# First samples loaded by phase, first taps by column halves, fewer direct outputs

## The chip, the cores and the metric

The kernel runs on one core of a Trainium2 chip. The metric is the time of one execution on the device in microseconds; a smaller one is better. Five engines work beside each other, each through its own queue of instructions in order: TensorE (PE), VectorE (DVE), ScalarE (ACT), GpSimd (POOL) and SyncE (SP), which only issues DMAs here. They wait for each other, and for DMAs, by semaphores.

## The reference

Inputs are `x` (2, 4000, 512), two convolutions' weights `w1` and `w2` (5, 512, 512), `g` (2, 8, 512) and three 512 x 512 matrices, all bfloat16.

```python
xp = jnp.pad(x, ((0,0),(2,2),(0,0)))
h = sum(einsum("btc,cd->btd", xp[:, i:i+T, :], w1[i]) for i in range(5))
h = gelu(h)[:, ::2, :]                       # 2000 positions a batch
hp = jnp.pad(h, ((0,0),(2,2),(0,0)))
f = sum(einsum("btc,cd->btd", hp[:, i:i+T1, :], w2[i]) for i in range(5))
f = gelu(f)[:, ::2, :]                       # 1000 positions a batch
fe = einsum("btd,de->bte", f, w_f)
ge = einsum("bud,de->bue", g, w_g)
j = tanh(fe[:, :, None, :] + ge[:, None, :, :])
return einsum("btud,dv->btuv", j, w_o)       # (2, 1000, 8, 512)
```

Only every second output of a convolution is kept. Output t of the first one is therefore made of five taps on the samples 2t-2 to 2t+2: taps 0, 2 and 4 read even samples, taps 1 and 3 read odd ones.

## The kernel before

Channels lie on the partitions in four blocks of 128, positions along the free dimension. The program is one long list of operations (`pl.op`, `pl.dma`), each with what it reads and writes and an estimated cost. `Plan.schedule` puts the list in order by simulating the engines with these costs, trying several hundred variants of the priorities on ACT and DVE; `Plan.emit` writes each engine's queue in that order and sets the waits. So an edit to a few operations can move others on DVE and ACT far from it. DMAs keep the order in which they stand in the list, and nearly all stand on SP's queue.

**First convolution, batch 0.** The outputs are made in two ways.

- *Direct*: the first `ND` = 438 outputs are the plain sum of five taps (`direct`, L778). The samples for it come untransposed: `load_xr` (L529, L533) loads blocks of 512 samples, four successive samples to a partition, 512 KB for the first block and 384 KB for the second. `turn` (L600, L609) transposes them on PE, 128 columns at a time, for one block `rt` and one phase `pp` (0 even, 1 odd), and DVE (L618) or ACT (L499) copies the result from PSUM into `eo`, which holds even and odd samples apart. Then each tap needs 16 matmuls (4 blocks of output channels by 4 of input channels), done in two pieces for taps 0, 4 and 2, columns up to 254 first and the rest when the second block is there, and in one piece for taps 1 and 3. The order of the taps is `TAPS = (0, 4, 2, 1, 3)`.
- *Triples* (`class Triple`, `class Unit`): three neighbouring outputs at a time out of 9 products and not 15, on sums and differences of sample planes and of weights. The first triple job of batch 0 covers `NF` = 186 triples (planes `xa` and `row`), the second 336 (`xp`); batch 1 has two of 334. The planes are loaded by transposing DMAs (`load_x6`, L543), one for each of six phases. ACT (L499) and DVE (L494) build the sums of planes, and `w1part` (L621, L494, L499) the sums of weights, `w_x` and `w_t`. It works in slices of 128 output channels, and its first step for a slice needs taps 0 and 4.

**After that** the second convolution runs on the same triples, then `fe` and `ge`, then ACT's tanh and the last matrix product. That is done in blocks of four tiles with seven products for eight (`class Seven`) and a few plain tiles (`class Plain`, L1063). Outputs leave as DMAs from SP and, at the very end, from ACT.

**The start.** PE first does `NWARM` = 7 matmuls on zeros. SP issues the first block of samples, tap 0, tap 4, then the second block when the first has landed, tap 2 when tap 0 has landed, and then `xa` planes 4 and 0, tap 1 (once tap 4 has landed), plane 2, tap 3 (once the second block has landed), planes 1, 3 and 5, and the twelve planes of the next two triple jobs. On PE the sixteen transposes of the first block, both phases, stand before the first direct matmul; tap 0 and tap 4 up to column 254 come next, then the sixteen transposes of the second block.

**The end.** The last operations are three plain tiles and the last product of the last block: one plain tile, the first half (256 columns) of another, the product, the third plain tile, and the other half, which ACT copies out of PSUM and stores from its own queue:

```python
Plain(plains[0]).go()
end = Plain(plains[2])
end.half(0, "dve", "sp")
seven[-1].p4(True)
Plain(plains[1]).go()
end.half(1, "act", "act")
```

Lines named L... in the profile are those of helpers: L507 is every matmul (`mm`), L494 every sum of two operands (`tt`), L499 every ACT operation (`act`), L525 every load of weights, L1034 and L1035 copies out of PSUM on ACT or DVE as the plan chooses, L1060 and L1050 the stores.

## Time and profile before

| What | Value |
|---|---|
| Median of 3 runs | 252.72 us (252.49 to 252.78) |
| Profiled execution, its own time | 252.61 us |
| Its span, first to last instruction | 250.8 us |
| PE busy | 246.1 us, 98% |
| DVE busy | 209.4 us, 84% |
| ACT busy | 211.1 us, 84% |
| POOL busy | 98.8 us, 39% |
| Direct matmuls (`acc<-eo,w_sb`) | 128, from 5.93 to 22.38 us |
| Matmuls of the first triple job | 144, `128x186`, from 22.38 us |
| First block of samples, issue to landing | 0.74 to 4.16 us |
| Tap 4, issue to landing | 1.65 to 8.39 us |
| First transposing load issued | 6.09 us |
| Last copy out of PSUM ends | 247.99 us |

A line of a timeline has the start and the length in us, the engine, the line of the kernel, the operation, the tile written and the tile read, the shape and the count; in brackets stands how long the engine had been idle and what ended that. A line of windows has the stretch, its length, the busy time of each engine with the number of instructions, the granted clock of TensorE, and the DMA engines' mean busy share and rate. Queues of DMA issues are marked with a q (SPq). Busy PE is not PE at its peak, since the ends of matmuls are modelled; the distance from start to start tells more.

### The profile page before, as it was taken

How to read it: one execution, taken by the hardware profiler on the slowest of the kernel's cores; microseconds unless marked ns; L12 is line 12 of the kernel's file. 1: busy time of each engine (PE TensorE's matmuls, PEld its weight loads, DVE VectorE, ACT ScalarE, POOL GpSimd, SP SyncE). 2: the span in 40 equal slices, each digit the busy share in tenths (PEclk: the TensorE clock that was granted, in tenths of full speed). 3: DMA queues.
4: the chain of work that ended last, by engine and by line, in shares of the span. 5: the costliest groups of instructions: out<-in, count | busy, mean ns of one | idle time of the engine just before them, and what ended most of it. 6: DMA issues, size and time to landing. Idle time of an engine off the chain costs nothing.

```text
span 250.8 us, 5265 instructions
## 1 busy us (share of the span) xinstructions
PE 246.1 (98%) x1947; PEld 183.4 (73%) x1947; DVE 209.4 (84%) x354; ACT 211.1 (84%) x351; POOL 98.8 (39%) x106
## 2 busy tenths in 40 slices
PE   8999999999999999999999999999999999999994
PEld 4887887666666666667556878777788878787882
DVE  2699998966999999398966888777999999987783
ACT  3399998859868867884599999999999999998772
POOL 1000000000000000000006978979799899888840
PEclk9999999999999999999999999999999999999999
DMA  7999999989000043000001043423354554555456
GB/s 241 276 242 195 158 197 179 187 208 293 2 3 0 0 146 109 0 4 0 0 3 42 0 137 111 132 86 104 94 184 142 187 188 158 167 173 185 151 189 210
DMA packets 54455, 31.86 MB, mean 127 GB/s; under 512 B 31390, under 2 KB 54206, under 8 KB 54430
## 3 DMA queue, kind: packets, MB, share of 16 engines
q1 hardware_dynamic: 54142, 31.34, 47.2%
q8 instruction: 15, 0.25, 0.4%
q10 hardware_dynamic: 288, 0.20, 0.3%
q14 instruction: 10, 0.08, 0.1%
HBM read 7.73 MB, written 16.38 MB: 96 GB/s over the span
## 4 chain that ended last, share of the span: by engine, by line
PE 93%; DMA 3%; ACT 2%; DVE 1%; issue 1%; SPq 0%; DVEq 0%
PE acc L507 92%; DMA w_sb<-in_w_dram 3%; ACT row L499 1%; DVE row L494 0%; PE acc L609 0%; DVE acc L621 0%; DVE w_t L494 0%; ACT w_x L499 0%; ACT sd L499 0%; SPq L525 0%; SPq L533 0%; ACT ost L499 0%; DVE sd L494 0%; DVEq L330 0%
## 5 line engine op out<-in xcount | busy, mean ns | idle before, releaser
L494 DVE TENSOR_TENSOR og<-acc,sn 128x512 bf16<-128x512 f32 x84 | 54.9, 682 | 7.9 <-PE acc L507 7.5
L499 ACT ACTIVATE jT<-feT,geT 128x1000 bf16<-128x1000 f32 (+5 forms) x60 | 57.4, 1016 | 0.3 <-DVE feT L494 0.3
L1108 POOL TENSOR_TENSOR ss<-jT 128x512 f16<-128x512 bf16 x33 | 38.4, 1170 | 41.3 <-DVE ss L1108 41.0
L507 PE MATMUL acc<-tw,ss 128*128 128x256 f16 x336 | 46.2, 273 | 0.0
L507 PE MATMUL acc<-row,w_sb 128*128 128x334 bf16 (+2 forms) x224 | 38.9, 296 | 0.2 <-DVE acc L621 0.2
L507 PEld LDWEIGHTS acc<-tw,ss 128*128 128x128 f16 x336 | 32.3, 98 | 7.6 <-ACT sn L1034 0.6
L507 PE MATMUL acc<-wo_sb,jT 128*128 128x256 bf16 (+1 forms) x208 | 33.2, 285 | 0.0
L1034 ACT ACTIVATE sn<-acc 128x512 f32<-128x512 f32 x48 | 29.7, 628 | 3.1 <-PE acc L507 2.3
L1035 DVE COPY sn<-acc 128x512 f32<-128x512 f32 x36 | 24.6, 685 | 7.0 <-PE acc L507 6.6
L507 PEld LDWEIGHTS acc<-row,w_sb 128*128 128x128 bf16 x224 | 21.1, 97 | 9.9 <-DVE acc L621 1.4
L491 POOL MEMSET hT<- 128x8 bf16 (+2 forms) x6 | 0.8, 148 | 63.2 <-ACT hT L499 46.3
L507 PEld LDWEIGHTS acc<-wo_sb,jT 128*128 128x128 bf16 x208 | 20.3, 98 | 5.0
L499 ACT ACTIVATE sd<-acc 128x334 f32<-128x334 f32 (+2 forms) x48 | 20.5, 432 | 2.9 <-PE acc L507 1.7
L499 ACT ACTIVATE hT<-acc 128x334 bf16<-128x334 f32 (+3 forms) x36 | 15.4, 438 | 8.7 <-PE acc L507 8.4
L1108 POOL TENSOR_TENSOR ss<-ss,jT 128x512 f16<-128x512 f16 x19 | 21.9, 1156 | 0.8 <-DVE ss L1108 0.8
L621 DVE SCALAR_TENSOR_TENSOR acc<-acc,sd 128x334 f32<-128x334 f32 (+2 forms) x24 | 11.5, 479 | 9.6 <-PE acc L507 9.5
L494 DVE TENSOR_TENSOR row<-row 128x1336 bf16<-128x1336 bf16 (+2 forms) x24 | 18.8, 792 | 0.0
L499 ACT ACTIVATE jX<-feT,geT 128x1000 bf16<-128x1000 f32 (+3 forms) x20 | 18.4, 968 | 0.0
L507 PE MATMUL acc<-xp,w_t 128*128 128x334 bf16 (+1 forms) x96 | 17.6, 305 | 0.0
L507 PE MATMUL acc<-hT,w_t 128*128 128x334 bf16 x96 | 17.6, 304 | 0.0
L507 PE MATMUL acc<-wo_sb,ss 128*128 128x256 bf16 x112 | 17.3, 273 | 0.0
L507 PE MATMUL acc<-xp,w_x 128*128 128x334 bf16 (+1 forms) x96 | 16.9, 305 | 0.0
(124 smaller groups left out, 494.6 us busy)
## 6 DMA issues: line engine op xcount, KB each, us to landing
out_dram<-og SPq DMA_DIRECT2D x42, 256.0 KB, 2.5
w_sb<-in_w_dram SPq DMA_DIRECT2D x10, 512.0 KB, 5.4
out_dram<-og SPq DMA_DIRECT2D x14, 128.0 KB, 2.1
out_dram<-ost SPq DMA_DIRECT2D x10, 128.0 KB, 1.9
xr<-in_x_dram SPq DMA_DIRECT2D x1, 512.0 KB, 3.4
wf_sb<-in_w_f_dram SPq DMA_DIRECT2D x1, 512.0 KB, 3.8
wg_sb<-in_w_g_dram SPq DMA_DIRECT2D x1, 512.0 KB, 4.8
wo_sb<-in_w_o_dram SPq DMA_DIRECT2D x1, 512.0 KB, 7.2
```

Source lines behind the costliest of these rows:

```text
L491: pl.op("pool", lambda e: e.memset(v.ap, 0.0), (), (v,))
L494: pl.op(eng, lambda e: e.tensor_tensor(out=o.ap, in0=a.ap, in1=b.ap, op=op), (a, b), (o,), 0.02 + 2.14e-3 * o.ap.free_size() if eng == "po ...
L499: pl.op("act", lambda e: e.activation(o.ap, i.ap, func, scale=scale, bias=0.0 if bias is None else bias.ap), rd, (o,), o.ap.free_size() * ...
L507: ins = e.matmul(o.ap, lhsT=l.ap, rhs=r.ap, start=start and n == 0, stop=stop and n == len(pairs) - 1, skip_group_check=not check)
L621: pl.op(eng, lambda e: e.scalar_tensor_tensor(out=o.ap, in0=a.ap, scalar=f, in1=b.ap, op0=ALU.mult, op1=add), (a, b), (o,), vec_cost(o, (a ...
L1034: pl.flex({"act": (lambda e: e.activation(o.ap, v.ap, ACT.Copy), 0.05 + n * 0.833e-3), "dve": (lambda e: e.tensor_copy(out=o.ap, in_=v.ap) ...
L1035: "dve": (lambda e: e.tensor_copy(out=o.ap, in_=v.ap), 0.065 + n * 1.04e-3)}, (v,), (o,))
L1108: fn = lambda e, o=S[i], x=x, y=y, op=op: e.tensor_tensor(out=o.ap, in0=x.ap, in1=y.ap, op=op)
```

## The change

The change has four parts.

1. The first samples come by phase: `load_xr` takes a phase and loads the two even, or the two odd, of the four samples on a partition. SP issues the even half of the first block first; the odd halves of both blocks come after tap 2. `turn` reads only its own phase. On PE the transposes of the odd phase stand behind the first pieces of taps 0, 4 and 2 and the second piece of tap 0. Only one of the copies into `eo` is DVE's; the others are ACT's.
2. Taps 0 and 4 come in column halves by turns: tap 0 left, tap 4 left, tap 0 right, tap 4 right, 256 KB each in rows of 512 bytes where rows had 1024. New waits on SP: the fourth piece waits for the first samples to land, the even half of the second block and tap 2 for the second piece, the odd halves for the fourth piece.
3. `ND` goes from 438 to 378 and `NF` from 186 to 206, so 60 direct outputs become 20 triples. The second block of samples shrinks from 96 partitions to 64. `NWARM` goes from 7 to 5, with two more such matmuls after the first eight transposes.
4. At the end the last plain tile is cut at column 384 and not 256, and the tile before it is multiplied and copied by DVE in two halves and stored in one DMA.

The planner sets the order anew: on DVE the weight sums of slice 3 come earlier, on ACT the copies of the odd phase stand between the first and the second operation on `xa` planes, and on PE the triples of the first two jobs are interleaved a little differently. From the second convolution on the queues have the same operations in nearly the same order, up to the end.

```diff
-    ND, NF = 438, 186
+    ND, NF = 378, 206
-    NWARM = 7
+    NWARM = 5
-        def load_xr(rt, after=None):
+        def load_xr(rt, pp, after=None):
             n = NR[rt]
-            dst = xr[rt].rows(0, n).map(lambda a: a.rearrange("p r k c -> p (r k c)"))
-            src = x[0, 4 * P * rt:4 * (P * rt + n), :].rearrange("(p r) c -> p (r c)", r=4)
-            o = pl.dma("sp", lambda e: e.dma_start(dst.ap, src), (), (dst,), nbytes=n * 4096, rate=370e3)
+            dst = xr[rt].rows(0, n, slice(pp, 4, 2)).map(lambda a: a.rearrange("p r k c -> p r (k c)"))
+            src = x[0, 4 * P * rt:4 * (P * rt + n), :].rearrange("(p r) c -> p r c", r=4)[:, pp:4:2, :]
+            o = pl.dma("sp", lambda e: e.dma_start(dst.ap, src), (), (dst,), nbytes=n * 2048, rate=350e3)
...
-        came = [load_xr(0)]
+        came = [load_xr(0, 0)]
...
-        def load_w1(i, after=None):
-            o = load_w("sp", w1_sb[i], w1[i].rearrange("(k c) d -> c k d", c=P))
+        def load_w1(i, after=None, cl=slice(0, D)):
+            dst, src = w1_sb[i, :, cl], w1[i].rearrange("(k c) d -> c k d", c=P)[:, :, cl]
+            o = pl.dma("sp", lambda e: e.dma_start(dst.ap, src), (), (dst,), nbytes=P * NK * 2 * (cl.stop - cl.start))
...
-        came.append(load_w1(TAPS[0]))
-        came.append(load_w1(TAPS[1]))
-        came.append(load_xr(1, came[-3]))
-        came.append(load_w1(TAPS[2], came[-3]))
+        halves = slice(0, D // 2), slice(D // 2, D)
+        for cl in halves:
+            for i in TAPS[:2]:
+                first = load_w1(i, came[0] if cl.start and i else None, cl)
+            came.append(first)
+        came.append(load_xr(1, 0, came[1]))
+        came.append(load_w1(TAPS[2], came[1]))
+        for rt in range(NX):
+            load_xr(rt, 1, came[2])
         load_a(4, 0)
...
-                pl.op("pe", fn, (xr[rt][:], ident[:]), (pv,), cost)
+                pl.op("pe", fn, (xr[rt][pp:4:2], ident[:]), (pv,), cost)
...
-                if h or rt:
+                if h or rt or pp:
                     act(o, v, ACT.Copy)
...
         turn(0, 0, 0.43)
+        pl.hold = [max(o.idx for o in pl.ops if o.eng == "pe")]
+        warm_mm(2)
+        pl.hold = []
         direct(TAPS[0], 0, NH)
-        turn(0, 1, 0.43)
         direct(TAPS[1], 0, NH)
         turn(1, 0, 0.17)
+        direct(TAPS[2], 0, NH)
+        direct(TAPS[0], NH, ND)
+        turn(0, 1, 0.43)
         turn(1, 1, 0.17)
-        direct(TAPS[2], 0, NH)
-        for i in TAPS[:3]:
+        for i in TAPS[1:3]:
             direct(i, NH, ND)
...
-            def half(self, h, eng, queue):
-                self.part(slice(h * H, (h + 1) * H), eng, queue)
+            def halves(self, eng, queue):
+                for cl in (slice(0, H), slice(H, NT)):
+                    bk = take()
+                    v = ps.cols(bk * NT, H)
+                    mm(v, [(jcols(k, self.jt * P, P), wo_sb[k, cl]) for k in range(NK)], True, True)
+                    evict(eng, ost[self.s][cl], v)
+                    free.append(bk)
+                store(self.jt, lambda a, b: ost[self.s].rows(a, b), ("p", self.s), queue)
...
-        end.half(0, "dve", "sp")
+        end.part(slice(0, 3 * P), "dve", "sp")
         seven[-1].p4(True)
-        Plain(plains[1]).go()
-        end.half(1, "act", "act")
+        Plain(plains[1]).halves("dve", "sp")
+        end.part(slice(3 * P, NT), "act", "act")
```

## The prediction

> **What bounds the kernel now.** I read the page first, for the share of each engine:
>
> ```profile
> span 250.8 us, 5265 instructions
> ...
> PE 246.1 (98%) x1947; PEld 183.4 (73%) x1947; DVE 209.4 (84%) x354; ACT 211.1 (84%) x351; POOL 98.8 (39%) x106
> ```
>
> PE has hardly any idle time, so a gain has to be less PE work or an earlier PE. Next the chain that ended last, in order of time:
>
> ```profile
> 1.65 6.74 DMA w_sb<-in_w_dram
> 8.39 0.05 issue
> 8.43 1.92 PE acc L507 x16
> ...
> 24.41 1.32 ACT row L499
> ...
> 31.31 216.28 PE acc L507 x1676
> 247.59 0.02 issue
> 247.61 0.38 ACT ost L499
> ```
>
> The start is a load of weights (tap 4, landed at 8.39), a stretch shared with ACT and DVE follows, and from 31.31 PE alone sets the end. What PE gains before 31.31 moves the end if ACT, DVE and the loads keep up. PE's timeline of the start:
>
> ```profile
> 1.19 3.17 PE L507 MATMUL acc<-zero 128*128 128x512 bf16 x7 [1.19 <-DVE zero L514]
> 4.21 1.89 PE L609 MATMUL acc<-ident,xr 128*128 128x128 bf16 x16
> 5.93 4.42 PE L507 MATMUL acc<-eo,w_sb 128*128 128x254 bf16 x32
> 10.19 0.84 PE L609 MATMUL acc<-ident,xr 96*128 96x96 bf16 x16
> 10.87 11.67 PE L507 MATMUL acc<-eo,w_sb 128*128 128x254 bf16 x96
> 22.38 1.13 PE L507 MATMUL acc<-xa,w_x 128*128 128x186 bf16 x12
> ```
>
> Direct outputs run from 5.93 to 22.38, then triples. Windows of a quarter of a microsecond, PE alone, the number of matmuls in brackets:
>
> ```profile
> 6.75:7.00 0.25, 0.25 (x3) 1.00 1.34 389
> 7.25:7.50 0.25, 0.25 (x5) 1.00 1.11 172
> ```
>
> The same 254-column matmul starts every 0.212 us up to 7.0 and every 0.109 us after it: PE runs at half rate until about 7.0, though the clock column reads 1.00. Last, the queue that issues the loads, SP:
>
> ```profile
> 5.66 0.38 SPq L525 DMA_DIRECT2D w_sb<-in_w_dram  x1
> 6.09 3.28 SPq L543 DMA_TRANSPOSE xa<-in_x_dram  x2
> 9.41 0.58 SPq L525 DMA_DIRECT2D w_sb<-in_w_dram  x1
> 10.04 1.22 SPq L543 DMA_TRANSPOSE xa<-in_x_dram  x1
> ```
>
> Each transposing load holds SP for 1.2 to 2.3 us, and SP issues without a pause from 5.66 to 39: what is put ahead of 6.09 pushes all that follows.
>
> **The change, part by part.** The sum is against the profiled execution, 252.61 us (span 250.8), 0.11 under the median of 252.72.
>
> *A, first direct matmul.* The 512 KB of first samples landed at 4.16, and the first direct matmul came 1.77 later: two groups of four transposes (0.107 us each), then ACT's copy, 5.28 to 5.88. That lag stays, since the first eight transposes, one DVE and one ACT copy are what it consists of. Only 256 KB has to land now. In half-microsecond windows the DMA moved 0.36 MB by 3.0 and 0.53 MB by 3.5, so 0.26 MB by 2.75; the landing came 0.65 after the bytes with its slowest engine and 0.1 with its fastest, so the half lands between 2.9 and 3.5; I take 3.25. The five warm-up matmuls end at 3.3, and the first direct matmul starts at 5.03: -0.9 (-1.1 to -0.6).
>
> *B, half rate.* From 5.93 to 7.0 half rate cost 0.53; from 5.03 it costs 0.98 if PE speeds up at the same time. +0.45, half of A in any case.
>
> *C, wait for tap 4.* PE stood still 0.22 before 8.43. By halves the four pieces are 512 packets of 512 B each. The trace has such packets at the end, in stores: 28.5 ns, against 46 ns for 1024 B. One piece takes 512/16 x 28.5 = 0.91, so they land near 4.2, 5.1, 6.0 and 6.9 (as loads: between 0.74, half a 1024-byte tap, and 1.1). PE takes tap 0 whole and then tap 4, so it asks for the first and third piece at 5.0 and 6.7 and for the second and fourth at 7.8 and 8.7. Without a straggler none is late: -0.22, and no new wait.
>
> *D, PE work.* 80 direct matmuls lose 60 columns: 4800/2400 = -2.0. 144 triple matmuls (9 products x 4 x 4) gain 20: +1.2. The eight odd-phase transposes of the first block move behind A and run at full rate: +0.45; the sixteen of the second shrink from 96 to 64 columns, 0.0425 us each before the change and 0.028 to 0.0425 after it, taken at no gain. Sum -0.35 (-0.6 to -0.35).
>
> *E, PE's waits for DVE and ACT.* 0.17 before 26.25 and 0.23 before 31.31. DVE works without a break from 8.41, when tap 4 landed, to 40.07. Now it can start at 5.1, 3.3 earlier, while PE reaches the triples about 2 earlier (F). About twelve planes grow by 10%: 0.04 us each on DVE (0.54 for 744 elements), 0.07 on ACT (0.81), 0.4 on either. The phase-1 copy moved from DVE was in DVE's idle time and takes ACT 0.6. On ACT four late copies of the odd phases now stand between its first and second xa plane and hold the second back to about 14.4. DVE comes to its first operation on a plane after fourteen weight operations of 0.6, at 13.6; it needs the second xa load there, which lands at 13.5 to 14.6 (F), and all its plane work queues behind that: up to 1.0 late. The first product of the triples needs ten more of its operations, at 19.4 to 20.4; PE asks at 20.1. POOL only clears edges here. The waits get smaller or stay: -0.2 (-0.4 to +0.4).
>
> *F, SP.* Four DMAs more (0.4 us of SP each), and waits for landings: the fourth weight piece for the first samples, the second block for the second piece, the odd phases for the fourth. Behind the last stand all xa planes, taps 1 and 3, and the xp planes. It ends at 6.9, or 7.8 if one of the sixteen DMA engines is late as in tap 4 (fifteen done at 7.53, the last at 8.39). Two issues on, the transposes start at 7.8 to 8.7 and not at 6.09. The second xa load goes out 1.4 after them and holds SP 1.9; the last one landed 2.6 after its issue, so this one lands at 13.7 to 14.6 at most, 13.5 if its issue is as short as the others'. Tap 1, issued 3.3 after the first (9.41 - 6.09), goes out at 11.1 to 12.0; a 512 KB load on quiet queues took 3.8 (wf_sb, median in the page), so it lands at 14.9 to 15.8. PE wants it at 15.0: 5.03 + 32 x 0.109 + 0.98 + transposes 0.34 + 16 x 0.109 (tap 2) + 16 x 0.0545 + transposes 0.79 + 32 x 0.0545, with 124 columns at 0.0545. Tap 3 follows 1.9 later and lands at 16.8 to 17.7; PE wants it at 17.6. Every DMA stood still 1.3 us near 15.6 in the trace; if it falls in here, tap 3 costs up to 1.2. No gain is possible from a queue that starts later. +0.3, from 0 to +2, nearer the low end since both estimates meet what PE wants.
>
> By the Trainium skill, page "DMA: Bandwidth & Descriptors", Specifications, 512 B is the smallest transfer at line rate; the rows here do not agree (18 B per ns against 22 for 1024 B). By that rule each piece would take 0.74, the fourth would land near 6.2, and the sum would be 0.3 lower, F being 0.
>
> *G, the end.* PE's last piece, four matmuls of 256, ends at 247.57; ACT copies 0.38, and its DMA goes out at 248.02. A 128-column copy takes about 0.28, so that store goes out 0.1 earlier. But the tile before it is copied by DVE in two halves of 0.42, the second starting when the first ends, and SP sends it at 0.42 after PE's end, not 0.32; it took 2.05 to land. -0.05 (-0.2 to +0.2, 256-byte rows being slow at worst).
>
> Sum: -0.9 + 0.45 - 0.22 - 0.35 - 0.2 + 0.3 - 0.05 = -0.97. 252.61 - 0.97 + 0.11 = 251.75, so 251.8.
>
> **Rivals.**
> 1. *SP becomes the bound* (slower). If the fourth piece lands after 8.3, the transposing loads start after 9.1, tap 1 lands after 16.1 and costs 1.2, and the gain is gone; with the pause tap 3 costs 0.6 more, and the xp planes, which ACT took 2.4 to 2.9 after they landed, come 3 late to an ACT that is 1 early, half a microsecond or so of which reaches PE. F = 2.3, E = +0.2: 254.1. For it: tap 4's straggler, and the odd phases wait for that very piece. Against: 1.3 MB stand before it up to its landing, where 1.5 MB did before tap 4's.
> 2. *No change.* The landing of the first half is latency and not bytes (3.6: A and B together +0.2 worse) and one pause or straggler costs 0.7 in F: 252.7. For it: the first 4 KB packets took 0.6 us, later ones 0.16.
> 3. *Full rate comes late* (slower). Before, PE sped up 5.8 after its first matmul. If the shorter warm-up, five matmuls and then two after the transposes, makes that count start anew with the first direct matmul, PE speeds up at 5.03 + 5.8 = 10.8 and not at 7.0, and loses half of 3.8: 253.7. Against: PE's idle time up to 5.0 is at most 0.2, as before. The Trainium skill, page "TensorE: Matmul & The Clock Gate", Part 1, has a free-running window of about 3.4 us of activity that releases the clock; the 5.8 here agrees with one window that began half used. By that rule the switch could come a window later, at 10.4, which would give 253.5.
> 4. *A full gain.* PE speeds up by 5.0, or the pieces land as fast as 0.74: 251.1.
>
> **How the numbers follow.** The forecast, 251.2 to 252.2, gets 0.48; rival 1 0.14, rival 2 0.24, rival 3 0.05, rival 4 0.09. Range 251.1 to 253.5: it takes in rivals 2, 3 and 4 and leaves rival 1's worse half and a better gain outside. A measurement of this kernel tells 0.2%, 0.5 us, from no change. Faster (under 252.2): forecast and rival 4, 0.56; within: 0.25; slower: 0.19.
>
> **What would show it.** A: transposes at 3.3 and the first direct matmul near 5.0. B: matmuls 0.212 apart until 7.0. C: no gap in the first 32. D: triples of 206 columns at 0.088 each. E: DVE at work from about 5.1, and PE's waits up to 31 under 0.4. F: SP's first transposing load at 7.8 to 8.7, PE's waits before tap 1 and tap 3 under 0.5 together. G: the end 3.2 after PE's last matmul. I am wrong if PE stands still over a microsecond between 9 and 20, if its waits move to the triples, or if the half of the samples lands with the time of the whole.

## The result and the profile after

The changed kernel takes 254.81 us (median of six, 253.89 to 255.35), the kernel before on the same chip 252.96 (252.49 to 253.46). The ratio is 1.0075, 95% interval 1.0055 to 1.0094: slower by 1.9 us, where 1.0 us less was forecast (251.8 against 252.72). All profiles below are of one execution each; for the changed kernel 254.65 us, 2.04 above the profiled execution of before.

The first lines of the changed kernel's page, span and share of the engines:

```profile
span 252.8 us, 5292 instructions
...
PE 245.2 (97%) x1951; PEld 183.1 (72%) x1951; DVE 210.7 (83%) x354; ACT 210.6 (83%) x352; POOL 98.9 (39%) x106
```

PE is busy 0.9 us less than before, and the span is 2.0 us longer: PE has gained idle time. Its timeline shows where (columns: start, length, engine, line, operation, and in brackets the idle time ahead of the group with what ended it):

```profile
1.19 2.31 PE L507 MATMUL acc<-zero 128*128 128x512 bf16 x5 [1.19 <-DVE zero L514]
3.98 1.04 PE L615 MATMUL acc<-ident,xr 128*128 128x128 bf16 x8 [0.48 <-DMA xr<-in_x_dram]
4.81 1.06 PE L507 MATMUL acc<-zero 128*128 128x512 bf16 x2
5.71 4.13 PE L507 MATMUL acc<-eo,w_sb 128*128 128x254 bf16 x32
9.77 0.40 PE L615 MATMUL acc<-ident,xr 64*128 64x64 bf16 x8
10.92 2.79 PE L507 MATMUL acc<-eo,w_sb 128*128 128x254 bf16 x32 [0.75 <-DMA w_sb<-in_w_dram]
13.55 0.94 PE L615 MATMUL acc<-ident,xr 128*128 128x128 bf16 x16
14.42 1.96 PE L507 MATMUL acc<-eo,w_sb 128*128 128x124 bf16 x32
18.05 5.32 PE L507 MATMUL acc<-eo,w_sb 128*128 128x378 bf16 x32 [1.67 <-ACT w_x L499]
```

The direct stage starts 0.22 earlier (5.71, before 5.93), waits 0.75 for tap 2 and stands still 1.67 in front of tap 1. The bracket of that last wait names ACT, by the event that came last; but the matmuls of tap 1 read no result of ACT that is this new (ACT's last copy into `eo` ended at 15.84). By the landings of its sixteen parts, tap 1 was complete at 17.91, and that is what PE waited for. It was issued at 11.71, as the queue SP shows:

```profile
6.14 0.60 SPq L533 DMA_DIRECT2D xr<-in_x_dram  x1
6.79 0.58 SPq L550 DMA_DIRECT2D w_sb<-in_w_dram  x1
7.73 1.22 SPq L533 DMA_DIRECT2D xr<-in_x_dram  x2
8.99 2.67 SPq L543 DMA_TRANSPOSE xa<-in_x_dram  x2
11.71 0.58 SPq L550 DMA_DIRECT2D w_sb<-in_w_dram  x1
```

The windows from 14 to 18 (busy time by engine, granted clock, share and rate of the DMA engines) show why it took 6.2 us to land:

```profile
14.00:15.00 1.00, 1.00 (x22) 0.86 (x20) 1.00 (x3) 1.00 (x3) 0.00 (x0) 1.00 0.90 265
15.00:16.00 1.00, 1.00 (x22) 1.00 (x20) 1.00 (x3) 1.00 (x4) 0.00 (x0) 1.00 2.22 354
16.00:17.00 1.00, 0.38 (x7) 0.20 (x4) 1.00 (x3) 1.00 (x2) 0.00 (x0) 1.00 1.25 28
17.00:18.00 1.00, 0.00 (x0) 0.00 (x0) 1.00 (x2) 0.92 (x2) 0.00 (x0) 1.00 0.33 67
```

From 16 to 18 the transfers moved 28 and 67 GB/s. Twenty packets of the transposing loads, 256 bytes each, started between 15.97 and 16.49 and were not done until 17.7 to 17.8; below this is called a standstill. DVE and ACT worked on.

Put together by stages, changed kernel against before, from the starts of the groups (each difference is of the two profiled executions, rounded, so that the rows ahead of the first triple make 0.9 where the starts differ by 0.83):

| step | us |
|---|---|
| first direct matmul, 5.93 to 5.71 | -0.22 |
| first 32 matmuls (wait for tap 4, half rate), 4.26 to 4.06 | -0.20 |
| waits for tap 2 (with the tail of the transposes) and for tap 1 | +0.9 and +1.8 |
| 80 direct matmuls with 60 columns less | -1.75 |
| transposes (0.79 to 1.07) and 0.1 in tap 2's matmuls | +0.4 |
| first triple, 22.38 to 23.21 | +0.83 |
| from the first triple to the end, 230.23 to 231.44: 1.2 of columns; 0.15 less of waits in the triples, as much more elsewhere | +1.21 |

So two things cost: what lies in front of the first triple is longer although it has less work, and the triples are longer by their columns.

### The profile page after: what moved, and what is told of

Its sections match the earlier page's. It is cut to its first block, busy times and chain, and to the rows that moved or that the text cites. A ratio compares the mean times of both kernels' runs of the same rounds, so it can differ in the third digit from the quotient of the medians.

```text
span 252.8 us, 5292 instructions
## 1 busy us (share of the span) xinstructions
PE 245.2 (97%) x1951; PEld 183.1 (72%) x1951; DVE 210.7 (83%) x354; ACT 210.6 (83%) x352; POOL 98.9 (39%) x106
## 4 chain that ended last, share of the span: by engine, by line
PE 70%; DVE 13%; ACT 8%; DMA 3%; issue 3%; SPq 1%; ACTq 0%; DVEq 0%
PE acc L507 70%; ACT row L499 4%; DMA w_sb<-in_w_dram 3%; DVE row L494 2%; DVE ws L627 2%; DVE ssum L494 2%; DVE hT L494 2%; ACT w_x L499 1%; DVE xp L494 1%; DVE sd L494 1%; DVE acc L627 1%; DVE w_sb L494 1%; ACT hT L499 1%; DVE w_t L494 1%; ACT sd L499 1%
## 5 line engine op out<-in xcount | busy, mean ns | idle before, releaser
L507 PE MATMUL acc<-row,w_t 128*128 128x334 bf16 (+2 forms) x96 | 16.7, 296 | 0.1
```

The source lines that it names most:

```text
L507: ins = e.matmul(o.ap, lhsT=l.ap, rhs=r.ap, start=start and n == 0, stop=stop and n == len(pairs) - 1, skip_group_check=not check)
```

## Experiments

Theory after the result: the lost time lies in the loads, which come later by the pieces, the odd halves and the waits on SP (F in the prediction). Rivals: the split of the outputs (378 and 206) itself costs; DVE and ACT set the pace of the triples; the standstill near 16 only happened to hit tap 1. All ratios are against the kernel before, timed on the same chip beside the kernel in question. "S" below is the start of the first triple, "rest" the profiled execution's time less S.

### The parts alone

The split alone, in the kernel before:

```diff
-    ND, NF = 438, 186
+    ND, NF = 378, 206
```

> The kernel before with 378 direct outputs and 206 triples in place of 438 and 186, nothing else. My theory: the split is worth what the sum says, 4800 columns of direct matmuls less (-2.0 us) and 144 x 20 columns of triples more (+1.2), and the lost time of the change lies in its loads. Tap 1 landed at 13.69 and tap 3 at 17.06; PE would come to them near 14.8 and 17.3, so neither is late: -0.8, ratio 0.997 (0.995 to 0.999). Rival, that the split itself costs (longer planes on DVE and ACT, which were at the limit before the triples): 0 to +0.8, and waits of PE for DVE or ACT of a microsecond in the triples.

Measured: 253.58 us, ratio 1.0029 (1.0011 to 1.0047). The forecast of 0.997 falls, and with it the idea that only the new loads cost. PE in the split alone:

```profile
8.88 1.92 PE L507 MATMUL acc<-eo,w_sb 128*128 128x254 bf16 x16 [1.19 <-DMA w_sb<-in_w_dram]
10.74 0.64 PE L609 MATMUL acc<-ident,xr 64*128 64x64 bf16 x16
11.31 4.57 PE L507 MATMUL acc<-eo,w_sb 128*128 128x254 bf16 x64
16.39 5.32 PE L507 MATMUL acc<-eo,w_sb 128*128 128x378 bf16 x32 [0.52 <-DMA w_sb<-in_w_dram]
21.69 1.25 PE L507 MATMUL acc<-xa,w_x 128*128 128x206 bf16 x12
22.92 1.23 PE L507 MATMUL acc<-row,w_x 128*128 128x206 bf16 x12
24.63 0.62 PE L507 MATMUL acc<-xa,w_x 128*128 128x206 bf16 x5 [0.48 <-DVE xa L494]
```

PE now comes to tap 1 at 15.87, ahead of its landing at 16.25, and waits for DVE in the triples. It also waited 1.19 for tap 4, which landed at 8.84 here (8.39 before). S is 21.69, 0.69 earlier than before; the rest takes 232.03, 1.8 more, of which 1.2 are columns.

The new loads alone, that is the changed kernel with the old split and the old end:

```diff
-    ND, NF = 378, 206
+    ND, NF = 438, 186
```

> The changed kernel's loads by phase and by column halves, its order of PE and its five and two warm-up matmuls, with the old 438 and 186 and the old end. My theory: the loads are what costs. PE waits for tap 2 by about 0.8 as in the changed kernel (landing near 10.9), and comes to tap 1 about 1.2 later than there, because the 48 matmuls ahead of it are 60 columns longer; tap 1 lands near 17.9, so that wait is 0.6 and not 1.7. Against before: -0.25 (start), -0.2 (tap 4), +0.8, +0.6, 0.2 for DVE and ACT: +1.0 to +1.4, ratio 1.004 to 1.006. Rival, that the loads are harmless by themselves and only the shorter direct stage makes them late: +0.2 or less.

Measured: 254.01 us, ratio 1.0048 (1.0031 to 1.0064): the sum is the theory's, its parts are not all. Tap 2 landed at 10.77 and PE waited 0.86; tap 1 landed at 17.23, and the wait for it shrank to about 0.2, where the theory had 0.6. The other 0.7 was a wait for DVE in the triples, where it had 0.2. So the loads cost 1.2 by themselves.

The new end alone, in the kernel before:

```diff
-        end.half(0, "dve", "sp")
+        end.part(slice(0, 3 * P), "dve", "sp")
         seven[-1].p4(True)
-        Plain(plains[1]).go()
-        end.half(1, "act", "act")
+        Plain(plains[1]).halves("dve", "sp")
+        end.part(slice(3 * P, NT), "act", "act")
```

> The kernel before with the changed kernel's end alone: one plain tile of output in 384 and 128 columns, another in two halves of 256. The traces of both kernels show the same lag at the last matmul (1.97 us) and at the last store, so the end is worth between -0.1 and +0.1: ratio 0.9995 to 1.0005. The rival, that the smaller pieces cost what the sum left out (four matmuls more and one more copy): +0.2 to +0.4.

Measured: ratio 0.9984 (0.9965 to 1.0004), which leaves the question open, so it was timed once more:

> The kernel before with the changed kernel's end alone, timed in more rounds. The first time it was 0.9984 (0.9965 to 1.0004), and its profile had the time not at the end (3.29 from the last matmul's end to the span's end, 3.23 before) but at the start, where tap 4 came without a straggler. If the end is worth nothing: 0.9995 to 1.0005. If the 0.4 us was real: 0.9985 or less.

Measured: 253.03 us, ratio 1.0000 (0.9982 to 1.0017). From the last matmul's end to the span's end the profiles have 3.27 us in both runs of the new end and 3.24 before. The end is worth nothing that these runs can tell.

Whole taps 0 and 4 in the changed kernel, so that the column halves go and all else stays:

```diff
-        halves = slice(0, D // 2), slice(D // 2, D)
-        for cl in halves:
-            ...
+        came.append(load_w1(TAPS[0]))
+        came.append(load_w1(TAPS[1]))
```

> The changed kernel with taps 0 and 4 loaded whole again, in place of column halves by turns; the loads by phase, the split and the end stay. The four pieces landed at 4.96, 6.12, 6.99 and 7.71, where rows of 1024 bytes at the speed of before would have brought the same megabyte by 7.0. Theory that the halves are the cause: tap 0 lands near 5.4 and tap 4 near 7.0, all that waits for them on SP goes out 0.7 earlier, tap 2 lands near 10.1 (no wait) and tap 1 is asked for at 11.0 and lands near 15, before the standstill of the transfers near 16: 2 us better than the changed kernel, ratio to before 0.998 to 1.001. Rival, that the waits on SP and the two odd halves ahead of the transposing loads are the cause: at most 0.7 better, ratio 1.004 to 1.007.

Measured: 253.74 us, ratio 1.0033 (1.0015 to 1.0051): the result between the two, 1.1 better than the changed kernel. Tap 4 was whole at 7.25 (the fourth piece at 7.71), but tap 2 landed at 10.66, hardly sooner than 10.87, and tap 1 at 16.95. The wait for it fell from 1.67 to 0.92.

The phases alone, which is the kernel of the new loads with whole taps again; the order of PE, the warm-up and the loads by phase stay, with the old split and the old end:

```diff
-        for cl in halves:
-            ...
+        came.append(load_w1(TAPS[0]))
+        came.append(load_w1(TAPS[1]))
```

> The first samples by even and odd phase alone, with the order of PE and the warm-up that go with it: whole taps, 438 and 186, the old end. The new loads with the old split gave 1.0048, and whole taps took 0.0042 off the changed kernel. If these add up, the phases alone are worth 1.0006 (0.999 to 1.002): the direct stage starts 0.2 earlier, and the wait of 0.6 for tap 2 takes it back. If the phases are the costly part (two loads more ahead of the transposing loads, rows of 1024 bytes where there were 4096): 1.003 or more, and the column halves next to nothing.

Measured: 253.9 us, ratio 1.0046 (1.0025 to 1.0067). The parts don't add up as assumed: the phases alone cost as much as phases and halves together (1.0048). In the profile tap 0 landed at 5.81 and PE waited 0.38 for it, 0.53 for tap 2 (10.56) and 0.41 for DVE later. That execution was the fastest of its eight, 0.6 under their median, so it shows less than what the phases cost.

### The waits on SP and the order of the loads

The changed kernel without the waits that hold a load back until an earlier one has landed (the same two lines in `load_xr` and in `load_w1`):

```diff
-            if after is not None:
-                o.after.append(after.idx)
```

> The changed kernel, with the waits taken away that hold a load on SP until an earlier load has landed (fourth weight piece, second block, tap 2, odd phases, taps 1 and 3); the order of the loads stays. In the changed kernel the transfers moved 31 GB/s between 7.0 and 7.25 and none between 7.25 and 7.5, because the second block went out only at 6.14, when the second piece had landed. Theory that these waits are the cause: SP issues tap 2 near 4.5 and tap 1 near 9, tap 2 lands near 9 and tap 1 near 14.5, both before PE asks for them (9.9 and 15.5): 2 us better than the changed kernel, ratio to before 0.997 to 1.001. Rival, that the bytes are the limit and transfers issued together only share what there is: the pieces land later by what tap 2 gains, PE starts on tap 4 late, ratio 1.005 or more.

Measured: 253.56 us, ratio 1.0023 (1.0003 to 1.0043). Taking the waits away gives back about 1.3 us of the 1.9, but not as the theory had it. SP issued tap 2 at 4.63 and tap 1 only at 11.37, since one transposing load held SP from 8.38 to 11.32; tap 2 landed at 11.12 and not at 9, the third piece at 7.80 and the fourth at 8.93. So the early loads came later, as the rival had it, and PE waited 1.09 in front of the third piece. The wait for tap 1 went, because it landed at 15.67, ahead of the standstill (17.71 to 19.10 here).

The same lines taken out of the kernel before:

> The kernel before, with the same waits on SP taken away, all else as it was. If the waits cost by themselves, the second block goes out at 2.1 and not at 4.18, tap 2 at 2.6 and the transposing loads at 3.1 in place of 6.09, and everything behind them comes 2 earlier; PE, which waited only 0.2 for a load there, gains at most that and the waits in the triples: ratio 0.997 to 0.9995. If transfers issued together share the bytes (rival), tap 4 lands later than 8.39 and PE loses: ratio 1.000 to 1.004.

Measured: 253.1 us, ratio 1.0001 (0.9983 to 1.0019). There the waits neither cost nor help: tap 4 landed at 8.84, PE waited 1.01 for it, and SP was held 4.59 by its second transposing load, so tap 1 went out at 10.15, later than with the waits.

The changed kernel with tap 1 ahead of the first two transposing loads:

```diff
-        load_a(4, 0)
         came.append(load_w1(TAPS[3], came[-3]))
+        load_a(4, 0)
         load_a(2)
```

> The changed kernel with tap 1 issued ahead of the first two transposing loads in place of behind them. It was issued at 11.71 and landed at 17.91, with a standstill of the 256-byte packets between 15.97 and 17.82 in between. Issued at 9.0 it should land near 13.5 (6.4 for 384 + 512 KB behind tap 2's 10.87 at 330 GB/s), and PE's wait of 1.67 goes; the two transposing loads land 0.6 to 1.5 later, and DVE's and ACT's first plane with them. If tap 1's place is the cause: 0.8 to 1.7 better than the changed kernel, ratio to before 1.001 to 1.005. If the planes are what bounds the triples in any case, the wait moves to the triples: less than 0.5 better, ratio over 1.0055.

Measured: 253.82 us, ratio 1.0041 (1.0023 to 1.0059), 0.9 better than the changed kernel; tap 1 landed at 13.90, the wait for it is gone, and one of 0.26 for tap 3 (19.15) came instead. That is the first of the two answers: tap 1's lateness was worth about a microsecond.

If the taps are what the shorter direct stage waits for, both taps should go first. In the split alone:

```diff
-        load_a(4, 0)
-        came.append(load_w1(TAPS[3], came[-3]))
-        load_a(2)
-        came.append(load_w1(TAPS[4], came[-3]))
-        load_a(1, 3, 5)
+        came.append(load_w1(TAPS[3]))
+        came.append(load_w1(TAPS[4]))
+        load_a(4, 0, 2, 1, 3, 5)
```

> The split alone (378 and 206, the loads and the end of before), and with it taps 1 and 3 issued ahead of all six transposing loads of the xa planes, without waiting. Theory: the direct stage can't end before tap 3 has landed and its 16 x 0.157 us are done; that is why 4800 columns less gave nothing. With tap 3 landing near 15 in place of 18.5, the direct stage ends where PE's own work ends, 20.2 to 20.9 instead of 21.7, and the 231.4 us that follow it with 206 triples give a time 0.8 to 1.5 under the split alone: ratio to before 0.997 to 1.000. Rival, that the triples then wait for planes that come 1.5 to 3 later: PE's waits move to the triples (over 0.8 there), ratio 1.001 to 1.004.

Measured: 253.71 us, ratio 1.0018 (1.0004 to 1.0033). PE in this kernel:

```profile
11.72 9.72 PE L507 MATMUL acc<-eo,w_sb 128*128 128x254 bf16 x96 [0.38 <-DMA w_sb<-in_w_dram]
21.98 1.24 PE L507 MATMUL acc<-xa,w_x 128*128 128x206 bf16 x12 [0.53 <-DVE xa L494]
23.56 1.27 PE L507 MATMUL acc<-row,w_x 128*128 128x206 bf16 x12 [0.34 <-DVE row L494]
```

Taps 1 and 3 landed at 13.19 and 14.64, the whole direct stage behind tap 2 ran without a wait, and the waits stood in front of the triples: 0.53, 0.34 and 0.54 from 27.4. The second plane had landed at 17.59, where the split alone had it at 12.77. The rival has it: the wait moves. With one plane between the two taps:

```diff
         came.append(load_w1(TAPS[3]))
+        load_a(4)
         came.append(load_w1(TAPS[4]))
-        load_a(4, 0, 2, 1, 3, 5)
+        load_a(0, 2, 1, 3, 5)
```

> The split alone, with taps 1 and 3 put ahead by less: tap 1, one xa plane, tap 3, the other five planes, without waiting. By the theory that tap 3's landing bounds the direct stage: tap 3 lands near 16, 2.5 earlier than in the split alone, the first plane 0.7 earlier than with both taps ahead; direct stage ends by 21, ratio to before 0.997 to 1.000, and the better of the two orders if the planes matter as well. By the rival (the planes bound): no better than the split alone, 1.002 to 1.004.

Measured: 254.12 us, ratio 1.0041 (1.0027 to 1.0055), no better than the split alone; a wait of 1.03 for DVE stands ahead of the first triple. And both taps first (the edit of the last kernel but one) in the changed kernel with whole taps:

> The changed kernel with whole taps 0 and 4 (as run before) and with taps 1 and 3 ahead of the six transposing loads. Same theory: tap 1 lands near 14 and tap 3 near 16, PE waits for neither (0.92 before); what is left are the waits for tap 0 (0.75) and tap 2 (0.64). The direct stage ends near 21.3 and the time is 0.9 under that of whole taps alone: ratio 0.999 to 1.001. Rival (planes): 1.003, with the wait in the triples.

Measured: 253.87 us, ratio 1.0032 (1.0016 to 1.0048), the same as whole taps alone. No wait for taps 1, 2 and 3 is left in its profile, and one of 0.76 for DVE ahead of the first triple (S 22.18) is.

### Without the loads of taps 1 and 3

Three kernels use tap 0 for tap 1 and tap 2 for tap 3, so that 1 MB is not loaded (which computes another convolution, with the same instructions on PE, DVE and ACT):

```diff
+        class Taps:
+            def __getitem__(self, idx):
+                ...
+                return w1_ld[({1: 0, 3: 2}.get(idx[0], idx[0]),) + idx[1:]]
...
-        came.append(load_w1(TAPS[3], came[-3]))
...
-        came.append(load_w1(TAPS[4], came[-3]))
```

> The kernel before without the loads of taps 1 and 3 (1 MB less ahead of the planes): wherever the program uses tap 1 it takes tap 0, for tap 3 it takes tap 2, so the convolution is computed with the wrong taps, and no instruction of PE, DVE or ACT is left out. It is the base for the next two. In the kernel before PE waited 0.2 for a load and 0.4 for DVE or ACT up to the triples' end: 0 to 0.6 us less, ratio 0.9975 to 1.000.

> The same without the loads of taps 1 and 3 (tap 0 and tap 2 in their places), with 378 and 206 in place of 438 and 186. Theory that the split's gain of PE work is real, and was lost because loads that have to land behind each other can't be brought forward: with 1 MB less it shows, -2.0 and +1.2, 0.8 under the kernel before without the same loads: ratio to before 0.994 to 0.997. Rival, that DVE and ACT set the pace of the triples whatever lands when: no better than the kernel before without these loads, 0.998 to 1.001.

> The changed kernel without the loads of taps 1 and 3 (tap 0 and tap 2 in their places). If these two loads' lateness is all that the changed kernel lost behind tap 2, the wait of 1.67 goes, and the triples lose little: 1.7 to 2.2 under the changed kernel, ratio to before 0.999 to 1.001, above the split alone without these loads by what tap 2 still costs (0.75). If more is lost by the new loads themselves (pieces and odd halves): 1.002 to 1.005.

Measured: 253.51 us, 1.0010 (0.9991 to 1.0029) for the kernel before; 253.41, 1.0025 (1.0007 to 1.0044) with the split; 252.88, 1.0001 (0.9989 to 1.0013) for the changed kernel. The last one says that the changed kernel loses 1.9 us to these two loads and what they hold up. The other two say that the split gives nothing even without them. In the split without these loads S is 20.73, the earliest of all, but the rest takes 232.64, 2.1 more than in the kernel before without them, where columns explain 1.2. The windows of before (first fence) and of the split without the two loads (second), from 9 to 22 and from 22 to 38:

```profile
9.00:22.00 13.00, 13.00 (x123) 10.07 (x121) 13.00 (x26) 11.24 (x21) 0.35 (x3) 1.00 1.13 237
22.00:38.00 16.00, 15.77 (x171) 13.95 (x170) 16.00 (x33) 15.40 (x33) 0.24 (x2) 1.00 1.13 182
```

```profile
9.00:22.00 13.00, 12.90 (x140) 10.05 (x138) 13.00 (x26) 9.62 (x19) 0.12 (x1) 1.00 0.99 181
22.00:38.00 16.00, 15.39 (x153) 12.86 (x151) 16.00 (x32) 14.24 (x28) 0.48 (x4) 1.00 1.05 191
```

The third figure behind the comma is DVE: 13.00 of 13 and 16.00 of 16 in both. From tap 4's landing to 38 DVE has no idle time in these two (in the changed kernel it stood still 1.9 between 9 and 38, 1.5 of it for loads). PE came to the triples 1.65 earlier than before. It waited there 0.26 for DVE and 0.22 for ACT, and a little at many products: by the spacing of its matmuls it stood still 1.8 up to 40, and 1.0 in the kernel before without the two loads.

### DVE's start

Then DVE's start should decide. The column halves alone bring it forward, since DVE's first weight operations need only a part of the columns of taps 0 and 4. In the kernel before, and the same with the split:

```diff
-        came.append(load_w1(TAPS[0]))
-        came.append(load_w1(TAPS[1]))
-        came.append(load_xr(1, came[-3]))
-        came.append(load_w1(TAPS[2], came[-3]))
+        halves = slice(0, D // 2), slice(D // 2, D)
+        for cl in halves:
+            for i in TAPS[:2]:
+                first = load_w1(i, came[0] if cl.start and i else None, cl)
+            came.append(first)
+        came.append(load_xr(1, came[0]))
+        came.append(load_w1(TAPS[2], came[1]))
```

> The kernel before with the column halves of taps 0 and 4 by turns alone: the first samples whole, 438 and 186, the old end. In the profiles so far DVE begins its work for the triples when tap 4 has landed (8.4 to 8.9 with whole taps behind the whole samples, 6.15 in the changed kernel) and then has no idle time up to 38; and the last of tap 4's sixteen parts is often 1 to 2 us behind the first. By halves, the second piece should land near 6.4 and DVE begin 2 us earlier, PE's waits for DVE (0.5) go and the wait for tap 4 too (0.2 to 1.6): ratio 0.996 to 0.9995. Rival, that rows of 512 bytes are slow (the four pieces came 0.8 to 1.0 late) and PE starts tap 0's second half late: 1.000 to 1.004.

> The same with 378 and 206. Theory that DVE's start set what the split could give: with it at 6.4 and not at 8.9, the triples wait at most 0.5 (1.1 to 1.8 in the split alone and without the loads of taps 1 and 3), and the split is worth -0.3 to -0.8 against the halves alone, less what tap 1 costs (0.5 in the split alone): ratio 0.996 to 0.999, the best version so far. Rival, that loads and planes come too late for the shorter direct stage in any case: 1.002 to 1.004, with the wait on tap 1 or on the planes.

Measured: 252.95 us, 1.0020 (1.0002 to 1.0039) for the halves alone, and 253.33, 1.0037 (1.0021 to 1.0053) with the split. DVE began at 6.17 and 6.45, as expected, and in the halves alone PE has no wait at all in the triples (0.4 before): the rest is the shortest of all, 229.4. But the start lost more. The fourth piece landed at 8.89, the second block at 10.47 and tap 2 at 11.65, so that PE waited for all of them (0.2, 0.62 and 0.25, and 0.34 for the third piece), and S came at 23.2. With the split, DVE stood still for tap 2 (the line of DVE's waits for weights: sum, times, longest; the longest is tap 2's):

```profile
DVE wu L625 <- DMA w_sb<-in_w_dram: 1.9, 2, 1.7
```

S was 21.49, the rest 231.96, 2.5 more than without the split. The theory that DVE's start alone set what the split could give falls: moved forward by 2 us, it was in good part taken back by the wait for tap 2.

The split, with and without, in all five pairs (the two last pairs are of different sessions and hold the new end too):

| surroundings | ratio without | ratio with | S without, with | rest without, with |
|---|---|---|---|---|
| before | 1 | 1.0029 | 22.38, 21.69 | 230.23, 232.03 |
| without taps 1 and 3 | 1.0010 | 1.0025 | 23.36, 20.73 | 230.56, 232.64 |
| halves | 1.0020 | 1.0037 | 23.21, 21.49 | 229.44, 231.96 |
| phases | 1.0046 | 1.0033 | 22.92, 22.24 | 230.34, 231.52 |
| phases and halves | 1.0048 | 1.0075 | 23.30, 23.21 | 230.55, 231.44 |

The mean is +0.0015, 0.4 us, where PE's own work is 0.8 less. With the intervals of the ten ratios taken as independent it is good to about 0.0011, so a gain of 0.8 us (0.0032) is excluded. In the first three pairs S comes early with the split, and the rest grows by 1.8 to 2.5; in the last two it grows by the 1.2 of the columns or less. What goes beyond the columns is PE standing still in the triples. By the spacing of its matmuls (gaps of over 0.06) that is 0.6, 1.0 and 0.0 up to 40 without the split in the first three pairs and 1.1, 1.8 and 1.1 with it; in the last two 0.9 and 0.9 without, 0.9 and 0.3 with it. An early S does not bring it by itself: in the changed kernel without the waits on SP and in the one with tap 1 first S is 21.97 and 21.77, and PE stands still 0.5 and 0.4.

### The instruction loads and the standstills

In every trace the transfers stand still at least three times before 45 us, for 1.2 to 2.2 us each. By the packets, each of the 16 KB loads of instructions on queue 8 lies close to one: in the changed kernel the loads start at 15.95, 28.48 and 42.83 and the standstills at 15.97, 28.83 and 43.15. To move the first one, the seven warm-up matmuls were made 28 shorter ones:

```diff
-            for i in range(n):
-                mm(ps.cols(0, NT), [(z, zz)], True, True)
+            zz = zero[0:P]
+            for i in range(4 * n):
+                mm(ps.cols(0, P), [(z, zz)], True, True)
```

> The changed kernel with its seven warm-up matmuls of 512 columns as 28 of 128: the same columns, 42 instructions more on PE ahead of the direct outputs. In six traces each 16 KB load of instructions on queue 8 (one per 256 instructions of PE) is followed within 0.6 us by a standstill of some 20 transposing packets of 1.3 to 1.8 us (15.95 and 15.97 in the changed kernel). If the load of instructions brings the standstill, 42 instructions fewer are left to the first boundary: load near 13.5, packets standing from 13.5 to 15.5, tap 1 landing 0.5 to 1.5 earlier, ratio to before 1.002 to 1.006. If the standstill comes by itself at that time (the rival), the load of instructions moves to 13.5 and the packets still stand at 16.0 to 17.8, ratio unchanged at 1.0075.

Measured: 253.95 us, ratio 1.0041 (1.0025 to 1.0057), 0.9 better than the changed kernel. But the profile doesn't bear out the reason: the load moved to 14.10, and the standstill came at 16.26 to 17.59, 2.2 later and not at once; tap 1 landed at 17.71, hardly earlier than 17.91, and PE waited 0.71 for it because it came later itself. The experiment leaves it open what gained the 0.9; the profiled execution, 254.37, was the slowest of the ten. Over all twenty traces, the kernel before's included, the first load starts between 12.68 and 16.32 and the first standstill with it between 13.2 and 17.71. From 0.1 ahead to 2.2 behind each of the sixty loads, ten or more packets of at most 4 KB start that take over 0.8 us. Of stretches of the same length between 8 and 45 that touch no such load, 8 in a hundred have as many (near 10 to 11 and 31 to 34, for instance). That is company, not yet a cause.

What a standstill does to tap 1 the traces do show. In thirteen of the twenty profiled executions tap 1 goes out right behind two transposing loads. In seven of them it landed ahead of the first standstill with an instruction load, 4.2 to 4.3 after its issue (issued at 9.41 and landed at 13.69 before; at 11.37 and 15.67 in the changed kernel without waits, where the standstill came at 17.71). In the other six (the changed kernel, the split alone, the new loads, whole taps, the phases and the short warm-up) the standstill came first: tap 1 took 5.5 to 6.2 and landed 0.1 to 0.2 after the standstill's end. So the standstill did not just happen to lie there: it hits a tap 1 that the change issues 2.3 later. At 4.3 from its issue, tap 1 would have landed in the changed kernel at 16.0, and PE came to it at 16.2. That is an estimate, since no run is without the standstill.

## Why the prediction was wrong, by its steps

The sum said -0.97, and the two profiled executions lie +2.04 apart, 3.0 away from it. F has 2.4 of that (by the starts of the groups 2.7, forecast 0.3), A to C together 0.25, D 0.2, E and G 0.1.

- *A, first direct matmul: right mechanism, wrong size.* -0.22, forecast -0.9. The lag of 1.77 from the landing held to the hundredth (3.94 to 5.71). The half of the samples landed at 3.94 and not at 3.25: that is nearly the time of the whole (its 512 KB came at 4.16), the sign of being wrong that the prediction had named; rival 2 had 3.6. By the packets, the first one started at 2.22, and at 1.76 before: SP took 0.70 to issue the load (0.39 before), and 0.15 more passed after that. The 256 KB then took 1.32, where the 512 KB before took 2.03 and their first half 1.18. So the bytes did get less, and the way to the first packet, which the step had left as it was, got longer. The rest is the step's reading of the bytes: by the packets' ends the first 0.26 MB of before were there at 2.94, not at 2.75.
- *B, half rate.* The rate doubled at 6.7, and not at 7.0 as before; A and B together gave -0.25, forecast -0.45: the 0.2 that rival 2 took off.
- *C, the pieces.* The wait before tap 4 went, as forecast. The price per piece held: from 4.96 to 7.71 there are three pieces of 0.92 in the mean (forecast 0.91; one by one 1.17, 0.87 and 0.72). All four were 0.8 to 1.0 late, because A's landing was 0.7 late. From the samples' landing the megabyte took 3.77 by 512-byte rows (3.5 to 4.3 in the five kernels with these loads and waits) and 3.42 by 1024-byte rows (whole taps, 3.83 to 7.25; 3.4 to 3.55 in three kernels). So the shorter rows cost about a tenth in the mean. The packets point the same way: two of 512 bytes took 54 ns in the median, one of 1024 bytes 46. The rule of the Trainium skill, page "DMA: Bandwidth & Descriptors", Specifications, by which 512 bytes are enough for line rate, gave 0.74 per piece in the prediction; these runs don't bear it out: 19 B per ns against 22.
- *D, PE's work: right, and of no use.* The direct matmuls lost 1.75 (forecast 2.0) and the triples gained their 1.2. But the sum counted both as time. The 2.0 lay in front of loads and of DVE's work, which had been hidden behind it: of five pairs, none gained the 0.8, and the mean is +0.4. In the changed kernel the loads took the room: without two of them it is 1.9 faster. But in the kernel before the split gains nothing without these two loads either. That DVE takes the room there is read from its busy time and from the waits for it; no run tested it. The prediction had the cover in its hands (tap 1 wanted at 15.0, DVE's products at 19.4 to 20.4, PE at 20.1) and priced the work as if all of it were on the path.
- *E, DVE and ACT: the number right, the reason incomplete.* In the changed kernel the waits in the triples fell by about 0.15 (forecast 0.2). Why they stay small is open. The new loads with the old split came to the triples as late (23.30) and waited 0.66 for DVE there, and in the kernels with the split that came early, single waits for DVE ran from none to 1.03.
- *F, SP: the step that failed.* Forecast +0.3, up to +2; measured 0.75 for tap 2 and 1.67 for tap 1, 2.4. Three errors. Tap 2 is missing in the step: it waits on SP for the second piece, which landed at 6.12 and not at 5.1, and landed at 10.87, while PE came at 10.0. SP's issues were priced at 0.4 and took 0.56 to 0.61, so that the first transposing load went out at 8.99 and not at 7.8 to 8.7; tap 1's issue (11.71) was still inside the forecast. And tap 1's landing was taken as issue plus 3.8, from a load on quiet queues. Behind two transposing loads it took 4.2 to 4.3 wherever no standstill came first, and with the standstill 6.2. The prediction had named the standstill and set it against tap 3 alone. Rival 1 had F at 2.3 with a chance of 0.14. Its condition, a fourth piece after 8.3, did not come about (7.71), though the transposing loads started nearly as late as it had them (8.99 and 9.1). That its size fits is in part luck: tap 2 and the standstill made it.
- *G, the end.* Forecast -0.05 and measured nothing, 1.0000 (0.9982 to 1.0017).
- *Rival 3* did not occur in the changed kernel's profile, but it is real. In the changed kernel without taps 1 and 3 the first 32 direct matmuls took 5.55 in place of 4.13:

```profile
6.16 5.55 PE L515 MATMUL acc<-eo,w_sb 128*128 128x254 bf16 x32 [0.35 <-ACT eo L507]
```

  PE ran at half rate there until 10.1. The page "TensorE: Matmul & The Clock Gate" of the Trainium skill, Part 1, has a free-running window of about 3.4 us. By that rule the prediction had worked out 10.4 for a switch one window later; this execution's 10.1 lies near it, 3.4 after the changed kernel's 6.7.

What stays open: which of the loads or DVE is last at the first triple differs from kernel to kernel, and no run here took work from DVE; why the phases alone cost as much as phases and halves together; what brings the standstills; and what the 28 short warm-up matmuls gained. No version was clearly faster than the kernel before.

## What to carry to other kernels

Before work is taken off the busiest engine in a stage, write down for that stage when each load lands and when each helper engine is done, and move the engine's whole schedule forward by the gain: work that covers a load or a helper is worth only the smallest of those margins, while work that is added in a later stage that the engine bounds alone is paid in full. Price a load by its place in the queue (what lies ahead of it, and whether a standstill falls in), not by the time that it took on quiet queues, and check every load behind a new wait, not only the ones that were tight before. A wait on a landing costs twice: the queue goes idle (0 to 31 GB/s at 7.0 to 7.5 here), and the next load has its way from issue to first bytes still to go (6.14 to about 7.5).

## What was not expected of the hardware

- Half the bytes landed 0.2 us earlier than the whole: 256 KB in 1024-byte rows at 3.94, 512 KB in 4096-byte rows at 4.16. SP's issue of the shorter rows was 0.3 longer.
- The moment at which PE's rate doubles differs between executions of nearly the same start: with seven warm-up matmuls in one row it came at 4.3 in the end alone and at 7.0 in the kernel before, with the changed kernel's five and two at 6.7 and, without the loads of taps 1 and 3, at 10.1. Over the twenty executions it came between 4.2 and 10.1. The end alone in its profile:

```profile
4.14 1.10 PE L609 MATMUL acc<-ident,xr 128*128 128x128 bf16 x16
5.77 3.90 PE L507 MATMUL acc<-eo,w_sb 128*128 128x254 bf16 x32 [0.53 <-DMA w_sb<-in_w_dram]
```

- Tap 4's sixteen parts land together in some executions (6.8 to 7.5 with a plane between the taps) and over more than two microseconds in others (6.69 to 9.37 without taps 1 and 3), with the same loads ahead.
- A standstill of the transfers goes with each 16 KB load of instructions, in sixty of sixty cases within 2.2 us, and its longest packet took 1.2 to 2.2 us; with column halves and the split it held 1024-byte packets (15.33 to 16.9), so it is not a matter of the transposing loads alone.
